# Attention with mixed heads and a two-layer network on one core: weight stores, x stores and norm's product change queues

## The chip, the core and the metric

The program runs on one core of a Trainium2 chip. The metric is the device time of one execution in microseconds (us). Five engines work from queues of their own and wait for each other through semaphores: TensorE (PE, with its weight loads PEld), VectorE (DVE), ScalarE (ACT), GpSimd (POOL) and SyncE (SP), which here only issues DMAs. GpSimd issues DMAs too, in the same queue as its arithmetic. Each queue is worked off in the order in which it is written.

## The reference

Four batches, 12 heads, 448 tokens, head size 64. Scores of all heads are mixed by a 12x12 matrix before the softmax and by another one behind it. The result, transposed to 1792 tokens x 768, goes through a two-layer network with a leaky activation. All of it is float32; the network's weights arrive as float64.

```python
scores = scale * np.matmul(q, k.transpose(0, 1, 3, 2))
scores = np.einsum('bhij,hg->bgij', scores, w_pre)
scores = scores - np.max(scores, axis=-1, keepdims=True)
attn = np.exp(scores)
attn = attn / (np.sum(attn, axis=-1, keepdims=True) + 1e-09)
attn = np.einsum('bhij,hg->bgij', attn, w_post)
return np.matmul(attn, v).astype(np.float32)
...
h = x @ w_in
g = np.maximum(h, 0.0) + alpha * np.minimum(h, 0.0)
return (g @ w_out).astype(np.float32)
```

## The kernel before

**Steps.** The attention is cut into 90 steps; the function `step(n)` writes the work of step n, for n from -1 to 94. In a step PE mixes the scores of 20 query rows over the heads (`mix`, L213), DVE takes their maxima (L215, once per step, so the instructions of this line count the steps), ACT takes the exponentials (L222), `norm` turns the sums of the step before into the second mixing matrix `r` (L229, L230 and the product L233, all on DVE), `post` (L246) mixes the result of two steps before with it, and `qk` (L185) makes the scores of a later chunk of queries in a tile `st`. Every few steps (8, 14, 20, 25, 29, 35, 41, 47 and so on) `pv` (L269, L283) multiplies by the values and leaves a piece of x in `xe`.

**Relays.** The scores are laid out anew on the way from `st` to six buffers `sr` by DMAs on SP's queue (L203, L206), three steps ahead of the `mix` that reads them.

**Conversion.** The weights are rounded from float64 to float32 in the kernel. `convert` works through 64 units (128x384 numbers each: 16 slices f, two matrices x, two halves), and each unit has five conversion operations: L60; L64 with L61 and L62 on GpSimd; L65; L66; L67. The others are DVE's. The first three of unit i stand ahead of the last two of unit i-1. GpSimd fetches the raw numbers into four buffers `cr` (L307) and a rounded half `ct` goes to the scratch `wsc` in DRAM by a store on SP's queue (L317). That store is kept in the list `ripe` and written by `flush` at the start of the next step, ahead of that step's relays. The fetch into the buffer that unit i leaves is written behind the unit's last operation.

**The network.** `moe(t)` is the network for batch t, in four phases. A phase runs through `l1` (first layer, L414, then `prelu` on DVE, L368 and L369) and `l2` (second layer, L448, added up on DVE in L383). Between the steps' own work `moe_work` writes as much of it as `PACE` says: matmuls worth 5000 ns in a step of the first phase. For each weight slice GpSimd loads the rounded numbers back (`load_w`, L352), ACT makes the high part (L360) and GpSimd the low part (L361). `load_w` writes further conversion operations on the spot while the slice that it needs isn't converted. The attention of batch t must be in DRAM (`x2`, stores L286) before `load_x` (L464, SP) fetches it and `split_x` (L474, L475, DVE) cuts it in two parts.

**Lead.** Up to step `ready[0]` = 26 there is no network work and each step holds `CONV_LEAD` = 6 conversion operations; behind it come `CONV_T0` of them in each step until all are done.

Of the kernel before, what the change touches and what calls it, by code (L numbers as in the profile page):

```python
# [8 lines left out]
F32 = mybir.dt.float32  # L9
# [5 lines left out]
ALU = mybir.AluOpType  # L15
# [31 lines left out]
CONV_LEAD, CONV_T0 = 6, 9  # L47
# [23 lines left out]
def talking_heads_prelu(ctx: ExitStack, tc: tile.TileContext, q, k, v, w_pre, w_post, mask, w_in, w_out, alpha, out):  # L71
# [154 lines left out]
    def norm(n):  # L226
        se = se_t.pop(n)
        s1 = sm.tile([128, 2], F32, tag="s1", name=f"s1{n}")
        nc.vector.tensor_scalar_add(s1, se, 1e-9)  # L229
        nc.vector.reciprocal(out=s1, in_=s1)  # L230
        r = rp.tile([128, 2, HP], F32, tag="r", name=f"r{n}")
        wf = wq.rearrange("p (o g) i -> p o (g i)", o=1)
        nc.vector.tensor_tensor(r, wf.to_broadcast([128, 2, HP]),  # L233
                                s1.rearrange("p (u o) -> p u o", o=1).to_broadcast([128, 2, HP]), ALU.mult)
        r_t[n] = r

# [53 lines left out]
    ripe = []  # L290

    def flush(upto=None):
        while ripe and (upto is None or ripe[0][0] <= upto or len(ripe) > 2):
            ripe.pop(0)[1]()
        now, later[:] = list(later), []
        for f in now:
            f()

    def convert():
        todo = [(f, x, c) for f in range(NFC) for x in range(2) for c in range(0, DM, CU)]  # L300
        raw_c = {}

        def fetch_c(i):
            if i < len(todo):
                f, x, c = todo[i]
                raw_c[i] = cvp.tile([128, CU], I64, tag="cr", bufs=4, name=f"cr{f}_{x}_{c}")
                nc.gpsimd.dma_start(out=raw_c[i], in_=(w_in, w_out)[x][f, :, c:c + CU])  # L307

        def unit(i):
            f, x, c = todo[i]  # L310
            raw = raw_c.pop(i)
            e = cvp.tile([128, CU], I32, tag="ce", name=f"ce{f}_{x}_{c}")
            t = cvp.tile([128, CU], I32, tag="ct", bufs=4, name=f"ct{f}_{x}_{c}")
            for j, op in enumerate(round_f64(nc, raw, e, t)):
                op()
                if j == 4:
                    ripe.append((step_now[0], lambda: (stored.add((f, x, c)), nc.sync.dma_start(  # L317
                        out=wsc[f, :, x * DM + c:x * DM + c + CU], in_=t.bitcast(F32)))))
                    fetch_c(i + 4)
                yield  # L320

        for i in range(2):
            fetch_c(i)
        yield
        n = len(todo)
        seq = []
        for i in range(n + 1):
            seq += [(i, 0), (i, 1), (i, 2)] if i < n else []
            seq += [(i - 1, 3), (i - 1, 4)] if i else []
        units = {}  # L330
        for i, j in seq:
            if j == 0:
                units[i] = unit(i)
            next(units[i], None)
            if i < 2 and j == 1:
                fetch_c(i + 2)
            yield

# [3 lines left out]
    soon = []  # L342

    def load_w(u, x):
        t, f = divmod(u, NFC)
        if t >= len(TB):
            return
        while not all((f, x, c) in stored for c in range(0, DM, CU)):
            converts(1)
            flush()  # L350
        w = (rip, rop)[x].tile([128, DM], F32, tag="r", name=f"wr{u}_{x}")
        nc.gpsimd.dma_start(out=w, in_=wsc[f, :, x * DM:(x + 1) * DM])  # L352
        wr_t[u, x] = w

# [45 lines left out]
    def moe(t):  # L400
# [3 lines left out]
        for what, G in order():  # L404
            fs = [FG * G + j for j in range(FG)]
            if what == "l1":
                pt = grab()
                for f in fs:
# [17 lines left out]
                    load_w(u + 4, 0)  # L426
# [40 lines left out]
    def split_x(t):  # L467
        a, N = TB[t]
        while step_now[0] < ready[t]:
            yield  # L470
        xs = xs_t[t] = xsp.tile([128, 2, NCC, N], F32R, tag="xs", name=f"xs{t}")
        for c in range(NCC):
            xr = xr_t.pop((t, c))
            nc.vector.tensor_copy(xs[:, 0, c, :], xr[:, :N])  # L474
            nc.vector.tensor_tensor(xs[:, 1, c, :], xr[:, :N], xs[:, 0, c, :], ALU.subtract)  # L475
            if c + 2 < NCC:
                load_x(t, c + 2)
            yield
# [20 lines left out]
    with tc.manual_schedule():  # L499
# [54 lines left out]
        conv_done, conv_steps = 0, NFC * 2 * 5 * (DM // CU)  # L554
# [10 lines left out]

        def moe_work(n, amount):
            nonlocal cur, budget
            budget += amount
            while budget > 0 and cur < len(TB):
                if tasks[cur] is None:  # L570
                    if n <= ready[cur]:
                        budget = 0.0
                        return
                    for _ in (nxt_x[cur] if cur in nxt_x else split_x(cur)):
                        pass
                    if cur == 1:
                        converts(conv_steps)
                        flush()
# [8 lines left out]
        def step(n):  # L587
# [6 lines left out]
            lead = n <= ready[0]  # L594
            pace = 0.0 if lead else PACE[min(cur, 2)]
            flush(n - 1)
            if live(n):
                mix(n)
            if n >= 0:
                relays(2 * (n + RA + 1), (nc.sync,))  # L600
            for f, *args in loads:
                f(*args)
# [22 lines left out]
            else:  # L625
                moe_work(n, pace * 0.5)
                converts(CONV_T0 // 2)
                moe_work(n, pace * 0.5)
                converts(CONV_T0 - CONV_T0 // 2)
            flush(n - 1)  # L630
            for t in range(len(TB)):
                if n == ready[t] - 1:
                    load_x(t, 0)
                    load_x(t, 1)
                if n == ready[t] and t == 0:
# [3 lines left out]
            if n == ready[0] - 5:  # L639
                for u in range(2):  # L640
                    for x in range(2):
                        load_w(u, x)
            if n == ready[0] - 2:
                for u in range(2):
                    split_w(u, 0)
                    load_w(u + 2, 0)
# [43 lines left out]
```

## Time and profile before

| | us |
|---|---|
| three runs | 992.94, 994.39, 999.21 |
| median | 994.39 |
| the profiled execution: its own time | 1000.09 |
| the profiled execution: span of the core | 998.30 |

The span is what the trace covers. It lies 1.79 us below that execution's own time and 3.91 us above the median of the runs. Times in the trace are counted from the start of the span. An instruction's row gives its start, its length and, in brackets, the idle time of its engine ahead of it with what ended that. The granted clock is TensorE's, as a share of 2.4 GHz.

### The profile page before, as it was taken

The page shows a single profiled execution, that of the slowest core. Times are in us where ns is not written, and L with a number is a line of the kernel's source. Part 1 is how long each engine was busy: PE and PEld are TensorE (multiplying, and loading weights), DVE is VectorE, ACT ScalarE, POOL GpSimd, SP SyncE. Part 2 cuts the span into 40 slices and gives each one's busy share as a digit, 9 for nine tenths or more (in the row PEclk, how much of TensorE's full clock was granted, in tenths as well). Part 3 has the DMA queues.
Part 4 walks back from the last instruction along what each step waited for, and adds up shares of the span by engine and source line. Part 5 has one row for each costly group of instructions (what it writes and reads, how often), then busy time and mean ns, then how long its engine had stood idle before and what let it go on. Part 6 is the DMA issues. An engine that isn't in the chain of part 4 may idle for free. (4 is left out here: it accounts for less than half of the span.)

```text
span 998.3 us, 27494 instructions
## 1 busy us (share of the span) xinstructions
PE 863.6 (87%) x11532; PEld 667.6 (67%) x11532; DVE 620.9 (62%) x1077; ACT 427.8 (43%) x780; POOL 488.9 (49%) x562
## 2 busy tenths in 40 slices
PE   6567747776978886997999989999999999999997
PEld 3235425445757654785787867777878888879997
DVE  4487947757987997744554544546655553654564
ACT  2255626513443442543555445554654545132231
POOL 6443634626556675451335434362533335367661
PEclk7699979967988997997999999999999999999999
DMA  6777877866666776454444464366534332544322
GB/s 185 184 241 215 244 211 227 234 205 179 194 180 198 224 214 180 140 161 147 156 136 136 123 163 128 117 181 195 167 116 122 118 106 80 160 127 125 111 80 72
DMA packets 79724, 161.73 MB, mean 162 GB/s; under 512 B 26276, under 2 KB 64304, under 8 KB 79600
## 3 DMA queue, kind: packets, MB, share of 16 engines
q0 software_dynamic: 21312, 90.58, 33.6%
q1 hardware_dynamic: 57432, 68.18, 21.1%
q8 instruction: 91, 1.49, 0.6%
q10 hardware_dynamic: 856, 1.21, 0.5%
q14 instruction: 33, 0.27, 0.1%
HBM read 97.62 MB, written 23.59 MB: 121 GB/s over the span
## 5 line engine op out<-in xcount | busy, mean ns | idle before, releaser
L361 POOL TENSOR_TENSOR ws<-wr,ws 128x768 fp32r<-128x768 f32 x128 | 237.1, 1853 | 294.2 <-ACT ws L360 287.0
L414 PE MATMUL p<-xs,ws 128*128 128x448 f32 x1152 | 261.7, 381 | 9.9 <-DVE xs L474 8.4
L448 PE MATMUL p<-g,ws 128*128 128x448 f32 x1152 | 253.5, 375 | 13.4 <-ACT e L222 5.9
L414 PEld LDWEIGHTS p<-xs,ws 128*128 128x128 f32 x1152 | 219.3, 194 | 55.5 <-issue 18.6
L448 PEld LDWEIGHTS p<-g,ws 128*128 128x128 f32 x1152 | 219.3, 193 | 50.0 <-ACT e L222 6.7
L215 DVE TENSOR_REDUCE nm<-p 128x2 f32<-128x896 f32 x90 | 97.6, 1085 | 115.4 <-PE p L213 115.4
L246 PEld LDWEIGHTS p<-r,e 64*64 64x64 f32 x5040 | 104.7, 139 | 81.7 <-issue 39.6
L252 ACT COPY at<-p 128x960 f32<-128x960 f32 x88 | 86.8, 987 | 168.5 <-PE p L246 168.4
L222 ACT ACTIVATE e<-p,nm 128x448 f32<-128x448 f32 x180 | 112.8, 635 | 100.8 <-DVE nm L215 68.5
L246 PE MATMUL p<-r,e 64*64 64x60 f32 x5040 | 109.6, 227 | 41.5 <-DVE xe L283 17.2
L360 ACT CAST ws<-wr 128x768 fp32r<-128x768 f32 x128 | 104.0, 843 | 95.8 <-issue 55.1
L185 PE MATMUL p<-k,q 64*64 64x448 f32 x768 | 110.8, 614 | 39.2 <-ACT st L189 13.4
L383 DVE TENSOR_TENSOR acc<-p,acc 128x896 f32<-128x896 f32 x84 | 91.0, 1086 | 61.0 <-PE p L448 60.9
L213 PE MATMUL p<-sr,wk 64*64 64x448 f32 (+1 forms) x720 | 106.8, 585 | 21.9 <-DMA sr<-st 16.2
L189 ACT COPY st<-p 128x896 f32<-128x896 f32 x95 | 84.5, 913 | 57.0 <-DMA sr<-st 26.9
L368 DVE TENSOR_SCALAR t<-p,alpha_sb 128x448 f32<-128x448 f32 x64 | 43.4, 678 | 97.0 <-PE p L414 97.0
L352 POOL DMA_DIRECT2D wr<-wsc x128 | 72.2, 564 | 39.3 <-POOL ws L361 34.1
L269 PEld LDWEIGHTS p<-at,v 64*64 64x64 f32 x2688 | 76.9, 134 | 11.2 <-issue 5.5
L269 PE MATMUL p<-at,v 64*64 64x120 f32 (+1 forms) x2688 | 78.9, 262 | 2.4 <-ACT st L189 1.8
L185 PEld LDWEIGHTS p<-k,q 64*64 64x64 f32 x768 | 30.2, 145 | 60.5 <-issue 18.5
L213 PEld LDWEIGHTS p<-sr,wk 64*64 64x64 f32 (+1 forms) x720 | 25.8, 137 | 64.5 <-issue 31.6
L61 POOL TENSOR_SCALAR ce<-ce 128x384 int32<-128x384 int32 x64 | 34.9, 546 | 50.4 <-DVE ce L60 48.6
(47 smaller groups left out, 670.1 us busy)
## 6 DMA issues: line engine op xcount, KB each, us to landing
wr<-wsc POOLq DMA_DIRECT2D x128, 384.0 KB, 3.8
sr<-st SPq DMA_DIRECT2D x332, 105.0 KB
cr<-in_w_in_dram POOLq DMA_DIRECT2D x32, 384.0 KB, 5.2
cr<-in_w_out_dram POOLq DMA_DIRECT2D x32, 384.0 KB, 4.7
wsc<-ct SPq DMA_DIRECT2D x64, 192.0 KB
xr<-x SPq DMA_DIRECT2D x24, 224.0 KB
out_dram<-acc SPq DMA_DIRECT2D x12, 448.0 KB
q<-in_q_dram POOLq DMA_DIRECT2D x54, 90.0 KB, 5.1
```

The source lines that it names most:

```text
L185: nc.tensor.matmul(pt[64 * cc:64 * cc + 64, r, :S], q_t[ci][h, (3 * cc + p) * cn + SR0 * cc:(3 * cc + p) * cn + SR0 * cc + 64], k_t[b, p][ ...
L213: nc.tensor.matmul(to[hf:hf + 64, u, :S], wk[r, :], g[r, :], start=True, stop=True)
L215: nc.vector.tensor_reduce(out=nm, in_=to[:, :, :S], axis=AX.X, op=ALU.max, negate=True)
L222: nc.scalar.activation(out=e_t[n][:, u], in_=m_t[n][:, u, :S], func=AF.Exp, bias=nm_t[n][:, u:u + 1], scale=1.0, accum_out=se_t[n][:, u:u ...
L246: nc.tensor.matmul(dst[:, :, HI * u:HI * u + HI], e[h, u, 64 * jb:64 * jb + 64], r[h, u].rearrange("p (h i) -> p h i", h=H), start=True, s ...
L252: nc.scalar.copy(at[:, :, col:col + 2 * GI].rearrange("p q (g i) -> p g q i", g=2), pt[:, :, :NS * GP].rearrange("p g (q i) -> p g q i", i ...
L269: nc.tensor.matmul(to[64 * t:64 * t + 64, r, cl * cn:(cl + 1) * cn], v_t[b, hx][pr, s, (2 * cl + t) * D:(2 * cl + t + 1) * D], a_t[pr, s, ...
L360: nc.scalar.copy(t[:, 0], w)
L361: nc.gpsimd.tensor_tensor(t[:, 1], w, t[:, 0], ALU.subtract)
L383: nc.vector.tensor_tensor(dst, pt[:, :, :N], dst, ALU.add)
L414: nc.tensor.matmul(pt[:, f % 2, :S], w[:, tw, c * 128:(c + 1) * 128], xs[:, tx, c, :], start=(j == 0), stop=(j == 3 * NCC - 1))
L448: nc.tensor.matmul(pt[:, d, :S], w[:, tw, (c + d) * 128:(c + d + 1) * 128], g[:, tg], start=(j == 0), stop=(j == 3 * FG - 1))
```

## The change

1. A rounded half is stored by GpSimd (`close`, L301 in the new file) instead of SP. The store and the fetch of the next raw numbers stand behind GpSimd's two exponent operations (L61, L62) of the unit that is begun next but one.
2. `norm` is written inside the function that writes the steps. While the first network phase lasts, its product runs on GpSimd (L575 in the new file).
3. `flush` now writes x's stores behind the step's relays, once in a step. `load_x` and `split_x` come one step later, and so does every network phase; for the later phases `load_x` is written at the first use.
4. Each step of the first phase holds 8 and 9 conversion operations by turns (4 + n % 2, then 4) instead of 9, and `ahead` loads first-layer weights three slices ahead instead of four while t is 0.

```diff
-CONV_LEAD, CONV_T0 = 6, 9
+CONV_LEAD, CONV_T0 = 6, 8
...
-    def flush(upto=None):
-        while ripe and (upto is None or ripe[0][0] <= upto or len(ripe) > 2):
-            ripe.pop(0)[1]()
+    def flush():
         now, later[:] = list(later), []
...
+            def close():
+                stored.add((f, x, c))
+                nc.gpsimd.dma_start(out=wsc[f, :, x * DM + c:x * DM + c + CU], in_=t.bitcast(F32))
+                fetch_c(i + 4)
+
             for j, op in enumerate(round_f64(nc, raw, e, t)):
                 op()
+                if j == 1 and shut:
+                    shut.pop(0)()
                 if j == 4:
-                    ripe.append((step_now[0], lambda: (stored.add((f, x, c)), nc.sync.dma_start(
-                        out=wsc[f, :, x * DM + c:x * DM + c + CU], in_=t.bitcast(F32)))))
-                    fetch_c(i + 4)
+                    shut.append(close)
                 yield
...
+    def ahead(upto):
+        while next_w[0] <= upto:
+            load_w(next_w[0], 0)
+            next_w[0] += 1
...
+                if G == NG2 - 1 and t + 1 < len(TB) and step_now[0] > ready[t + 1]:
+                    load_x(t + 1, 0)
+                    load_x(t + 1, 1)
...
-                    load_w(u + 4, 0)
+                    ahead(u + (3 if t == 0 else 4))
...
-        while step_now[0] < ready[t]:
+        while step_now[0] < ready[t] + 1:
             yield
+        for c in range(2):
+            if (t, c) not in xr_t:
+                load_x(t, c)
...
+            (nc.gpsimd if cur == 0 else nc.vector).tensor_tensor(r, wf.to_broadcast([128, 2, HP]),
+                                    s1.rearrange("p (u o) -> p u o", o=1).to_broadcast([128, 2, HP]), ALU.mult)
...
-            lead = n <= ready[0]
+            lead = n <= ready[0] + 1
...
-            flush(n - 1)
             if live(n):
                 mix(n)
             if n >= 0:
                 relays(2 * (n + RA + 1), (nc.sync,))
+            flush()
...
-                converts(CONV_T0 // 2)
+                converts(CONV_T0 // 2 + n % 2)
                 moe_work(n, pace * 0.5)
                 converts(CONV_T0 - CONV_T0 // 2)
-            flush(n - 1)
             for t in range(len(TB)):
-                if n == ready[t] - 1:
+                if n == ready[t] and t == 0:
                     load_x(t, 0)
                     load_x(t, 1)
-                if n == ready[t] and t == 0:
+                if n == ready[t] + 1 and t == 0:
                     for _ in split_x(0):
                         pass
```

**GpSimd in the lead.** GpSimd's queue in a stretch of the lead: `ce` are the exponents of a unit, `cr` its raw numbers, `ct` its rounded half, with the matrix (0 or 1) and the half (0 or 384) behind the name; `r` is norm's product. Before:

```order
L307 DMA cr_0_384_1105<-in_w_in_dram 128x384
L61 TENSOR_SCALAR ce_1_384_1107<-ce_1_384_1107 128x384
L62 TENSOR_SCALAR ce_1_384_1107<-ce_1_384_1107 128x384
L307 DMA cr_1_0_1116<-in_w_out_dram 128x384
L168 DMA q_125<-in_q_dram 64x2x90 x2
```

After:

```order
L575 TENSOR_TENSOR r_998<-wq,s_995 128x120
L61 TENSOR_SCALAR ce_1_0_1040<-ce_1_0_1040 128x384
L62 TENSOR_SCALAR ce_1_0_1040<-ce_1_0_1040 128x384
L301 DMA wsc<-ct_0_0_908 128x384
L292 DMA cr_0_0_1047<-in_w_in_dram 128x384
```

The fetches into `cr` stood ahead of the exponent operations of the unit that is begun next. They now stand behind them and behind a store, and each step's product stands between.

**DVE in step 41.** DVE's queue in the middle of step 41, up to the first activation of `prelu` (L368 before, L364 after). Before:

```order
L60 TENSOR_SCALAR ce_0_384_4484<-cr_0_384_4285 128x384
L64 TENSOR_SCALAR ct_0_384_4485<-cr_0_384_4285 128x384
L65 SCALAR_TENSOR_TENSOR ct_0_384_4485<-cr_0_384_4285,ct_0_384_4485 128x384
L66 SCALAR_TENSOR_TENSOR ce_0_0_4457<-cr_0_0_4252,ce_0_0_4457 128x384
L67 TENSOR_TENSOR ct_0_0_4458<-ct_0_0_4458,ce_0_0_4457 128x384
L60 TENSOR_SCALAR ce_1_0_4494<-cr_1_0_4455 128x384
L64 TENSOR_SCALAR ct_1_0_4495<-cr_1_0_4455 128x384
L65 SCALAR_TENSOR_TENSOR ct_1_0_4495<-cr_1_0_4455,ct_1_0_4495 128x384
L66 SCALAR_TENSOR_TENSOR ce_0_384_4484<-cr_0_384_4285,ce_0_384_4484 128x384
L67 TENSOR_TENSOR ct_0_384_4485<-ct_0_384_4485,ce_0_384_4484 128x384
L368 TENSOR_SCALAR t_10_4506<-p_128,alpha_sb 128x448
L369 SCALAR_TENSOR_TENSOR t_10_4506<-p_128,t_10_4506 128x448
```

After, from the last conversion operation of step 41 on:

```order
L67 TENSOR_TENSOR ct_0_384_4236<-ct_0_384_4236,ce_0_384_4235 128x384
L215 TENSOR_REDUCE nm_4428<-p_129 128x2
L571 TENSOR_SCALAR s_4436<-se_4375 128x2
L572 RECIPROCAL s_4436<-s_4436 128x2
L60 TENSOR_SCALAR ce_1_384_4497<-cr_1_384_4385 128x384
L64 TENSOR_SCALAR ct_1_384_4498<-cr_1_384_4385 128x384
L65 SCALAR_TENSOR_TENSOR ct_1_384_4498<-cr_1_384_4385,ct_1_384_4498 128x384
L66 SCALAR_TENSOR_TENSOR ce_1_0_4390<-cr_1_0_4217,ce_1_0_4390 128x384
L364 TENSOR_SCALAR t_10_4522<-p_131,alpha_sb 128x448
L365 SCALAR_TENSOR_TENSOR t_10_4522<-p_131,t_10_4522 128x448
L364 TENSOR_SCALAR t_11_4525<-p_131,alpha_sb 128x448
L365 SCALAR_TENSOR_TENSOR t_11_4525<-p_131,t_11_4525 128x448
```

Before, the rows ahead of L368 are the end of a run of 17 conversion operations in step 41, 13 of which `load_w` asked for, and `prelu` waits behind all of them. After, the same `prelu` falls in step 42 and four conversion operations stand between norm's reciprocal and it.

**SP at the first hand-over.** SP's queue around the hand-over of batch 0: stores of x (`x`<-`xe`), loads of it (`xr`<-`x`), relays (`sr`<-`st`). Before:

```order
L286 DMA x_57<-xe_1_2365 128x3x28
L464 DMA xr_0_2422<-x_57 128x448
L464 DMA xr_1_2424<-x_57 128x448
L317 DMA wsc<-ct_1_0_2167 128x384
L203 DMA sr_121<-st_2011 60x1x448 x2
L203 DMA sr_122<-st_2011 60x1x448 x2
L464 DMA xr_2_2497<-x_57 128x448
```

After:

```order
L275 DMA x_57<-xe_1_2363 128x3x28
L463 DMA xr_0_2487<-x_57 128x448
L463 DMA xr_1_2489<-x_57 128x448
L203 DMA sr_117<-st_2228 60x1x448 x2
L203 DMA sr_118<-st_2228 60x1x448 x2
L463 DMA xr_2_2570<-x_57 128x448
```

Before, a store of a rounded half and four relays stood between the first two loads and the third. After, no store of a rounded half is left on the queue, and all of it comes one step of relays later.

## Rows read from the trace of the kernel before

**Rows 1.** The page's slices: busy tenths of DVE, granted clock of PE.

```profile
DVE  4487947757987997744554544546655553654564
...
PEclk7699979967988997997999999999999999999999
```

**Rows 2.** Windows by stage: us, busy us of each engine, clock, DMA share, GB/s.

```profile
0.00:195.10 195.10, 130.42 (x2596) 75.26 (x2596) 131.32 (x294) 90.92 (x177) 96.31 (x163) 0.86 0.76 216
195.10:216.60 21.50, 12.43 (x88) 6.09 (x88) 11.27 (x23) 3.08 (x6) 6.50 (x11) 0.58 0.83 259
216.60:400.80 184.20, 145.09 (x1943) 111.95 (x1943) 161.28 (x269) 71.88 (x132) 114.50 (x147) 0.88 0.65 189
400.80:428.90 28.10, 28.10 (x350) 21.33 (x351) 18.31 (x31) 16.26 (x30) 10.89 (x10) 1.00 0.47 140
```

**Rows 3.** Waits of PE, 216.6 to 400.8: us in total, times, longest.

```profile
PE p L246 <- DVE xe L283: 17.2, 3, 9.4
PE p L185 <- DVE t L369: 11.7, 3, 6.0
PE p L448 <- ACT e L222: 5.9, 2, 4.2
```

**Rows 4.** DVE by line, 216.6 to 400.8: count, busy, mean ns, idle before.

```profile
L67 DVE TENSOR_TENSOR ct<-ct,ce 128x384 f32<-128x384 f32 x30 | 26.8, 893 | 0.8
L66 DVE SCALAR_TENSOR_TENSOR ce<-cr,ce 128x384 int32<-128x384 int32 x30 | 23.3, 777 | 4.5 <-POOL ce L62 4.5
L65 DVE SCALAR_TENSOR_TENSOR ct<-cr,ct 128x384 f32<-128x384 uint32 x30 | 22.6, 755 | 0.9
L60 DVE TENSOR_SCALAR ce<-cr 128x384 int32<-128x384 int32 x30 | 18.5, 615 | 0.8
...
L64 DVE TENSOR_SCALAR ct<-cr 128x384 int32<-128x384 int32 x30 | 13.0, 432 | 0.0
```

**Rows 5.** Timeline, DVE and GpSimd at 190 us: start, length, instruction.

```profile
190.34 2.44 DVE L66 SCALAR_TENSOR_TENSOR ce<-cr,ce 128x384 int32<-128x384 int32 x1
192.81 0.56 DVE L67 TENSOR_TENSOR ct<-ct,ce 128x384 f32<-128x384 f32 x1
...
190.51 1.84 POOL L361 TENSOR_TENSOR ws<-wr,ws 128x768 fp32r<-128x768 f32 x1
```

**Rows 6.** Timeline, PE in step 41.

```profile
396.15 1.77 PE L185 MATMUL p<-k,q 64*64 64x448 f32 x8 [5.96 <-DVE t L369]
```

**Rows 7.** DVE by line, 0 to 195.1: the product, the reuse of ct.

```profile
L64 DVE TENSOR_SCALAR ct<-cr 128x384 int32<-128x384 int32 x33 | 12.1, 365 | 8.4 <-DMA wsc<-ct 8.3
L233 DVE TENSOR_TENSOR r<-wq,s 128x120 f32<-128x120 f32 x25 | 7.1, 283 | 0.9
```

**Rows 8.** GpSimd by line, 216.6 to 400.8.

```profile
L361 POOL TENSOR_TENSOR ws<-wr,ws 128x768 fp32r<-128x768 f32 x22 | 41.5, 1887 | 22.4 <-ACT ws L360 16.3 <-DMA sr<-st 5.3
L62 POOL TENSOR_SCALAR ce<-ce 128x384 int32<-128x384 int32 x30 | 18.6, 619 | 2.5
...
L352 POOL DMA_DIRECT2D wr<-wsc x22 | 12.8, 580 | 8.8 <-POOL ws L361 4.8 <-DMA wsc<-ct 3.8 <-DMA x<-xe 0.3
```

**Rows 9.** Timeline: fetch of unit 21, unit 19's L62, first use (L60).

```profile
113.79 0.57 POOL L307 DMA_DIRECT2D cr<-in_w_in_dram  x1 [1.42 <-DVE ce L66]
...
115.23 0.70 POOL L62 TENSOR_SCALAR ce<-ce 128x384 int32<-128x384 int32 x1
...
122.58 0.36 DVE L60 TENSOR_SCALAR ce<-cr 128x384 int32<-128x384 int32 x1
```

**Rows 10.** DMA issues, 0 to 195.1: count, KB each, median us to landing.

```profile
cr<-in_w_in_dram POOLq DMA_DIRECT2D x18, 384.0 KB, 5.7
...
wsc<-ct SPq DMA_DIRECT2D x30, 192.0 KB
```

**Rows 11.** DMA issues, 216.6 to 400.8, the same fetch.

```profile
cr<-in_w_in_dram POOLq DMA_DIRECT2D x13, 384.0 KB, 4.9
```

**Rows 12.** Timeline of DVE at the first hand-over.

```profile
204.87 0.39 DVE L474 CAST xs<-xr 128x448 fp32r<-128x448 f32 x1 [4.30 <-DMA xr<-x]
```

More of the change, by code (lines that the diff above doesn't have):

```diff
@@ L224, in exp @@
         free(m_t.pop(n))
[L226 to L235, printed above, removed]
     def post(n):
@@ L288, in pv @@
                 in_=xe[:, :3 * cn].rearrange("p (c i) -> p c i", c=3)[:, :, o + skip:o + w]))
-    ripe = []
-    def flush(upto=None):
-        while ripe and (upto is None or ripe[0][0] <= upto or len(ripe) > 2):
-            ripe.pop(0)[1]()
+    def flush():
         now, later[:] = list(later), []
@@ L300, in convert @@
         todo = [(f, x, c) for f in range(NFC) for x in range(2) for c in range(0, DM, CU)]
-        raw_c = {}
+        raw_c, shut = {}, []
         def fetch_c(i):
@@ L337, in convert @@
             yield
+        for f in shut:
+            f()
     wr_t, wi_t, wo_t, g_t, xs_t, xr_t = {}, {}, {}, {}, {}, {}
     nxt_x, stored = {}, set()
-    soon = []
+    soon, next_w = [], [0]
     def load_w(u, x):
@@ L349, in load_w @@
             converts(1)
-            flush()
         w = (rip, rop)[x].tile([128, DM], F32, tag="r", name=f"wr{u}_{x}")
@@ L553, in talking_heads_prelu @@
         next(conv)
-        conv_done, conv_steps = 0, NFC * 2 * 5 * (DM // CU)
+        conv_done, conv_steps = 0, NFC * 2 * 5 * (DM // CU) + 1
         tasks = [None] * len(TB)
@@ L564, in converts, with norm @@
                     conv_done += 1
+        def norm(n):
+            se = se_t.pop(n)
+            s1 = sm.tile([128, 2], F32, tag="s1", name=f"s1{n}")
+            nc.vector.tensor_scalar_add(s1, se, 1e-9)
+            nc.vector.reciprocal(out=s1, in_=s1)
+            r = rp.tile([128, 2, HP], F32, tag="r", name=f"r{n}")
+            wf = wq.rearrange("p (o g) i -> p o (g i)", o=1)
+            (nc.gpsimd if cur == 0 else nc.vector).tensor_tensor(r, wf.to_broadcast([128, 2, HP]),
+                                    s1.rearrange("p (u o) -> p u o", o=1).to_broadcast([128, 2, HP]), ALU.mult)
+            r_t[n] = r
         def moe_work(n, amount):
@@ L570, in moe_work @@
                 if tasks[cur] is None:
-                    if n <= ready[cur]:
+                    if n <= ready[cur] + 1:
                         budget = 0.0
@@ L577, in moe_work @@
                         converts(conv_steps)
-                        flush()
                         cvs.close()
@@ L639, in step @@
             if n == ready[0] - 5:
+                ahead(1)
                 for u in range(2):
-                    for x in range(2):
-                        load_w(u, x)
+                    load_w(u, 1)
             if n == ready[0] - 2:
@@ L645, in step @@
                     split_w(u, 0)
-                    load_w(u + 2, 0)
+                ahead(2)
         for n in range(-1, NB + LAG + 3):
```

## The prediction

> **What bounds the kernel now.** I read the page's slices first [rows 1]. The clock falls below full speed in most of the first sixteen slices (400 us) and almost nowhere behind them, so TensorE is kept waiting there and bounds the rest. The windows by stage [rows 2] say by whom. From 216.6 to 400.8 us, the first network phase while weights are still being converted, DVE is busy 161.3 of 184.2 us and PE 145.1. In the 28.1 us behind it, with the conversions over, PE is busy all of the time and DVE 18.3. The lead, up to 195.1, is mixed: DVE 131.3, PE 130.4, with 0.76 of the DMA engines taken. The interval between maxima that holds the first hand-over, 195.1 to 216.6, is the emptiest, with PE 12.4 of 21.5 us at a clock of 0.58.
>
> The waits of PE in the first phase [rows 3] are all for DVE or for ACT, which waits for DVE: xe 17.2 us, prelu's t 11.7, exponentials 5.9. No relay and no weight is among them. So a gain from SP's queue, where the change moves most DMAs, can't be read from this stage, and one from DVE's order and load can.
>
> **The price of a conversion operation.** In this stage DVE's five operations take 893, 777, 755, 615 and 432 ns [rows 4], 694 ns in the mean, and there are 30 of each: 150 operations in 15 steps (27 to 41), ten a step, though nine are written. The rest came by load_w.
>
> **Part 1, the spread of the conversions.** By the code the lead of before holds 28 x 6 = 168 of the 320 operations. The new lead has one step more, 174 of 321 (one is the end of the list). The remaining 147 go into steps 28 to 45 at 8.5 a step and load_w asks for none, since it finds its slices stored: 8.2 a step over 18 steps against 10 over 15. That takes 1.8 x 0.69 = 1.25 us of DVE's time from each step. A step of before is 184.2 / 15 = 12.28 us; I take 11.03 for the new one, so the 18 steps last 198.5 us. They begin one lead step later than 216.6; DVE is busy 131.3 / 26 = 5.05 us a step in the lead [rows 2], so 221.7 us. That puts the maximum of step 46 at 420.2 us. Before it stands at 428.9, but the network is a step further there, 5.0 us of matmuls by PACE, so 423.9 is the like of it: -3.7 us. The average leaves out the worst step. In step 41 seventeen conversion operations stand ahead of prelu, and PE waits 5.96 us for its t [rows 6], with the low clock behind it (slice 16 stands at 7 tenths) [rows 1]. In the new order four stand there. I count -5 for that: the wait, less about 1 us since conversions reappear in steps 42 to 45. DVE has the room: 18.3 of 28.1 us were busy [rows 2], 4.6 us a step, and 8.5 x 0.69 = 5.9 more makes 10.5, below 11.03. Sum -9. Bounds: if DVE's 22.9 idle us of this stage (184.2 - 161.3) all went, the step would be 161.3 / 15 - 1.25 = 9.5, less than PE's 145.1 / 15 = 9.67, and 18 x 9.67 gives -28 in all. If nothing of the smaller load showed but the longer stretch, 18 x 11.6 gives +7.
>
> **Part 2, norm's product on GpSimd.** 51 products leave DVE, 283 ns each in the lead [rows 7]. What they cost GpSimd has no row. By size from L361 [rows 8], 120 of 768 elements of 1887 ns are 295 ns; the upper bound is L62, 619 ns, which has 384. What DVE pays for it does have one: while L361 runs on GpSimd (190.51, 1.84 us) L66 takes 2.44 us, against 0.56 for L67 right behind it, clear of L361 [rows 5]. So a product of two tiles on GpSimd holds up DVE's work between SBUF tiles for as long as it lasts, and the operations behind the reciprocal are such work. DVE wins 283 ns and loses 0 to 500. I take a gain of 0.05 us on the 40 or so that lie in DVE-bound steps: -2, range -11 to +9. GpSimd itself has room: 114.5 of 184.2 us [rows 2], and 15 x (0.45 + 1.7 stores of 0.58, the price of L352 in rows 8) adds 21 us. It is on the path only if its waits add up.
>
> The Trainium skill (SBUF — State Buffer, section SBUF: two separate sides) has this as a lock that one of the two engines holds for a whole instruction; L66 in rows 5 agrees. By that rule alone, with every product locked out against a waiting DVE for 0.3 us, part 2 would be about 0 instead of -2.
>
> **Part 3, the later fetch.** This is a cost. Before, the raw numbers of unit 21 are asked for at 113.79 and first used at 122.58, 8.8 us later [rows 9]. In the new order the fetch stands behind unit 19's L62, which ends at 115.93, and behind a store (0.58): 116.5, which leaves 6.1 us. The median landing in the lead is 5.7 [rows 10], and now 192 KB of a store lie directly ahead of the 384 KB in the same queue. Bounds of the landing: 5.7, and 5.7 x 1.33 = 7.6 if the queue is one line and half of the two share their time. I take 6.6. A shortfall x must be made up by the nine conversion operations between fetch and use, so each unit's five stretch by 5x/9. With x = 0.5 and about 20 units (the lead holds 35; the others lie in steps that wait for something else) that is +6; with x = 0 it is 0 and with x = 1.5 it is +17. In the first phase the operations are slower and the landing shorter, 4.9 [rows 11], so I count nothing there.
>
> The skill's same section warns that DMAs issued by GpSimd starve, since their descriptors can't be written while DVE holds the port. It would lengthen these landings and move the sum to the first rival. The trace doesn't bear it out: DVE is busier from 216.6 on (0.88 against 0.67 of the time) and the landing is shorter there [rows 2, 10, 11].
>
> **Part 4, SP without rounded halves.** DVE waited 8.3 us in the lead for stores to clear ct [rows 7], five times. The store now leaves as soon as GpSimd gets to it and ten operations ahead of the reuse, so the wait goes. Most of it fell in steps that waited for something else anyway: -3, range -8 to 0.
>
> **Part 5, the hand-over.** The stores of x, its loads and the split all move one step, so their distances stay. DVE waits 4.30 us for the first piece [rows 12]. The loads are now a step behind the loads of v that are issued in step 25: -1, range -4 to +3. In the later hand-overs SP gets to the load later, but DVE has idle time there; 0, range -3 to +3.
>
> **Sum.** -9 - 2 + 6 - 3 - 1 = -9. The durations are of an execution of 1000.09 us, 5.7 above the median of 994.39. The differences carry over, so 994.4 - 9 = **985 us**.
>
> **Rivals.** (a) **The fetch binds the lead.** If the landing in the lead, with a store ahead, exceeds 7.6 us, x is above 1.5, part 3 costs 17 us or more, and the sum is +2 to +6: about **999**, slower than before. For it: the margin of 6.1 is within 0.4 of the median. Against it: DVE stretches by itself when DMAs are late. It decides from x = 1.3 on. (b) **The first phase evens out.** If most of DVE's 22.9 idle us go with the runs of conversions, because PE no longer falls to the low clock (0.88 in this stage), part 1 is -20 and the time **974**. For it: PE's waits of 17.2 and 11.7 us are three long ones each, the mark of runs and not of a steady lack. Against it: the steps with pv remain uneven. (c) **Nothing comes of it.** GpSimd's product and stores push its L62 behind, DVE waits for it (4.5 us before, rows 4), and the lost time equals what the spread gives: **994**.
>
> **How the numbers follow.** One per cent, 9.9 us, is about what a measurement of this kernel tells from no change. Chances: the forecast 0.40 (979 to 991), (a) 0.20, (b) 0.22, (c) 0.18. Faster by over 1% (below 984.5): (b) and half of the forecast, 0.42. Slower by over 1% (above 1004.3): a part of (a) with the upper ends of parts 1 and 2, 0.12. Within: 0.46. The range 968 to 1003 takes in the cases' centres and most of the bounds of part 1 below and of part 3 above.
>
> **What would show it.** Right: L215 of step 46 near 420 us; no wait of PE for prelu's t above 3 us; the five DVE operations at 10 operations a step fewer than before and still near 0.69 us; no DVE wait for wsc; the hand-over a step later but as long. Part 3 shows as idle time of L60 released by the cr loads, 5 to 6 us more than before; 15 us more is rival (a). Wrong: L66, L65 or L60 in the lead well above their means of before would say that the product on GpSimd costs DVE more than it saves; idle time of L66 released by L62 is rival (c).

## The result and the profile after

The changed kernel takes 1006.65 us (median of 4 runs, 1001.82 to 1011.01), the kernel before 996.02 in the same comparison. The ratio is 1.0103, 95% interval 1.0071 to 1.0136: slower by 10 us, where 985 was forecast and 1003 was the upper end. The profiled execution took 1011.01 us, its span 1009.2. Ratios here and below are of fast runs alone (1000.83 us of o4_four_if_stored and 1100.07 and 4041.30 of b_spread_alone are left out), medians of all runs.

The windows by stage, which answer to [rows 2], with the same columns. The second fence holds the stretch behind step 46 of the kernel before, which [rows 2] don't have. The lead now ends with step 27, the hand-over is 197.2 to 217.1, and steps 28 to 45 fill 217.1 to 431.9.

```profile
0.00:192.50 192.50, 129.31 (x2580) 80.19 (x2582) 128.59 (x269) 91.06 (x176) 125.36 (x217) 0.86 0.74 218
...
217.10:431.90 214.80, 175.46 (x2244) 132.55 (x2244) 169.30 (x268) 84.17 (x156) 146.85 (x204) 0.91 0.61 178
431.90:1009.20 577.30, 551.03 (x6535) 456.36 (x6533) 300.87 (x462) 244.13 (x434) 263.46 (x239) 0.98 0.45 131
```

```profile
428.90:998.30 569.40, 547.52 (x6572) 452.99 (x6564) 298.66 (x465) 245.69 (x435) 260.68 (x232) 0.98 0.46 132
```

Step 28's maximum falls at 217.1, 4.6 us earlier than the 221.7 of the prediction. The lead is not where the time went. Then 18 steps take 214.8 us, 11.93 each, against a forecast of 11.03 and an upper bound of 11.6: 16 us too much in one stage. DVE is idle 45.5 us of it (214.8 - 169.30), against 22.9 of 184.2 before, though its load was to be the limit. Behind step 46 the rest is 577.3 us, 569.4 before; 5.0 of the 7.9 us is, by PACE, the step of network work that was put off.

So the stage is read again, by its waits. Waits in 217.1 to 431.9 of the changed kernel, mainly those of ScalarE and DVE (us in total, times, longest):

```profile
ACT e L222 <- DVE nm L215: 41.8, 8, 15.0
ACT ws L356 <- DMA wr<-wsc: 39.0, 6, 6.7
DVE g L371 <- ACT g L370: 31.6, 6, 6.1
...
PE p L447 <- ACT at L241: 19.3, 6, 3.8
...
DVE t L364 <- PE p L413: 4.3, 2, 4.0
```

The first row is the largest, but it isn't new: it stood at 36.2 us before, and most of its longest wait, 15.0, lies ahead of 217.1. The second row is the new one. ScalarE waits 39.0 us for loads of weights, six times. In the stage of before the same casts waited for GpSimd alone and never for a load, by their row for 216.6 to 400.8:

```profile
L360 ACT CAST ws<-wr 128x768 fp32r<-128x768 f32 x22 | 17.8, 844 | 8.4 <-POOL ws L361 8.4
```

DVE now waits for ScalarE's g, six times too. One of the six, in step 33, in the timelines of ScalarE, GpSimd and DVE (start, length, instruction, idle time ahead and what ended it):

```profile
282.69 0.85 ACT L356 CAST ws<-wr 128x768 fp32r<-128x768 f32 x1
290.10 0.83 ACT L356 CAST ws<-wr 128x768 fp32r<-128x768 f32 x1 [6.56 <-DMA wr<-wsc]
290.84 1.03 ACT L370 CAST g<-t 128x448 fp32r<-128x448 f32 x2
291.77 0.97 ACT L241 COPY at<-p 128x960 f32<-128x960 f32 x1
...
283.62 1.82 POOL L357 TENSOR_TENSOR ws<-wr,ws 128x768 fp32r<-128x768 f32 x1 [0.35 <-ACT ws L356]
285.37 0.60 POOL L343 DMA_DIRECT2D wr<-wsc  x1
...
285.17 1.08 DVE L379 TENSOR_TENSOR acc<-p,acc 128x896 f32<-128x896 f32 x1
291.43 2.42 DVE L371 TENSOR_TENSOR g<-t,g 128x448 fp32r<-128x448 f32 x2 [5.18 <-ACT g L370]
```

Read it from the load. It is issued at 285.37, behind GpSimd's L357 of the slice before, and the cast that reads it starts 4.7 us later, at 290.1. That cast is the next one on ScalarE's queue and has waited since 283.5. Behind it stand `prelu`'s two casts g (L370) and the copy of at (L241), which need nothing of that load. DVE has finished L379 at 286.25 and stands still 5.18 us for g, with norm's and the conversions' work queued behind L371. TensorE's wait for at (19.3 us, six times) is the end of the chain. The cause in the code is the last line of the change: `ahead(u + 3)` asks for a slice right behind the cast of the one before. `l1` takes the slices in pairs, and in all six cases nothing stands on ScalarE's queue between the two casts of a pair. With four ahead the load had a whole pair's time. The buffer is not what holds the load up: there are two by turns, L357 has just left the other one, and the row at 285.37 has no wait. Only the order in the code, the load behind `split_w`, puts it there; no run tried the load ahead of it.

The rows that answer to the prediction's other marks. First two of DVE's conversion operations in the stage, by line:

```profile
L66 DVE SCALAR_TENSOR_TENSOR ce<-cr,ce 128x384 int32<-128x384 int32 x30 | 24.1, 804 | 0.4 <-POOL ce L62 0.4
L67 DVE TENSOR_TENSOR ct<-ct,ce 128x384 f32<-128x384 f32 x30 | 23.9, 796 | 0.8
```

Then the lead, 0 to 192.5: TensorE's longest wait in sum, DVE by line, and GpSimd by line.

```profile
PE p L235 <- POOL r L575: 24.0, 11, 3.6
```

```profile
L66 DVE SCALAR_TENSOR_TENSOR ce<-cr,ce 128x384 int32<-128x384 int32 x32 | 25.7, 802 | 0.0
...
L60 DVE TENSOR_SCALAR ce<-cr 128x384 int32<-128x384 int32 x33 | 12.6, 382 | 30.1 <-DMA cr<-in_w_out_dram 16.2 <-DMA cr<-in_w_in_dram 13.4
```

```profile
L575 POOL TENSOR_TENSOR r<-wq,s 128x120 f32<-128x120 f32 x25 | 11.7, 468 | 19.3 <-DVE s L572 19.1
```

The operations of the stage cost what was assumed (804 and 796 ns; 777 and 893 in [rows 4]). The product takes 468 ns on GpSimd, not the 295 that I scaled from L361. L60 waits 29.6 us for raw numbers in the lead, three times the 9.8 of the kernel before (5.4 and 4.4, one wait each).

### The profile page after: what moved, and what is told of

Its sections match the earlier page's. It is cut to its first block, busy times and chain, and to the rows that moved or that the text cites. A ratio compares the mean times of both kernels' runs of the same rounds, so it can differ in the third digit from the quotient of the medians.

```text
span 1009.2 us, 27411 instructions
## 1 busy us (share of the span) xinstructions
PE 871.5 (86%) x11532; PEld 677.3 (67%) x11532; DVE 613.5 (61%) x1026; ACT 427.2 (42%) x780; POOL 546.2 (54%) x677
## 4 chain that ended last, share of the span: by engine, by line
PE 52%; DMA 17%; DVE 11%; POOL 8%; issue 6%; ACT 5%; SPq 1%; POOLq 0%; ACTq 0%; DVEq 0%
PE p L413 18%; PE p L447 16%; PE p L258 6%; PE p L213 4%; PE p L235 4%; DMA sr<-st 4%; DMA wr<-wsc 4%; POOL ws L357 3%; DMA cr<-in_w_out_dram 3%; PE p L185 3%; DMA xr<-x 3%; DVE nm L215 2%; ACT ws L356 1%; DVE g L371 1%; DMA cr<-in_w_in_dram 1%
## 5 line engine op out<-in xcount | busy, mean ns | idle before, releaser
L357 POOL TENSOR_TENSOR ws<-wr,ws 128x768 fp32r<-128x768 f32 x128 | 236.3, 1847 | 274.1 <-ACT ws L356 272.7
L447 PE MATMUL p<-g,ws 128*128 128x448 f32 x1152 | 259.8, 381 | 31.0 <-ACT at L241 20.6
L447 PEld LDWEIGHTS p<-g,ws 128*128 128x128 f32 x1152 | 221.4, 195 | 69.3 <-ACT at L241 25.4
L215 DVE TENSOR_REDUCE nm<-p 128x2 f32<-128x896 f32 x90 | 97.6, 1084 | 96.4 <-PE p L213 90.2
L241 ACT COPY at<-p 128x960 f32<-128x960 f32 x88 | 86.5, 983 | 140.3 <-PE p L235 140.1
L185 PE MATMUL p<-k,q 64*64 64x448 f32 x768 | 106.2, 588 | 20.5 <-DMA k<-in_k_dram 6.6
L379 DVE TENSOR_TENSOR acc<-p,acc 128x896 f32<-128x896 f32 x84 | 90.9, 1085 | 50.9 <-PE p L447 50.8
L364 DVE TENSOR_SCALAR t<-p,alpha_sb 128x448 f32<-128x448 f32 x64 | 43.4, 678 | 90.8 <-PE p L413 90.8
L258 PEld LDWEIGHTS p<-at,v 64*64 64x64 f32 x2688 | 81.7, 140 | 15.7 <-issue 5.9
L258 PE MATMUL p<-at,v 64*64 64x120 f32 (+1 forms) x2688 | 84.2, 272 | 6.3 <-ACT st L189 3.6
L371 DVE TENSOR_TENSOR g<-t,g 128x448 fp32r<-128x448 f32 x64 | 65.5, 1063 | 38.7 <-ACT g L370 38.7
L61 POOL TENSOR_SCALAR ce<-ce 128x384 int32<-128x384 int32 x64 | 35.5, 554 | 51.6 <-DVE ce L60 48.7
```

The source lines that it names most:

```text
L185: nc.tensor.matmul(pt[64 * cc:64 * cc + 64, r, :S], q_t[ci][h, (3 * cc + p) * cn + SR0 * cc:(3 * cc + p) * cn + SR0 * cc + 64], k_t[b, p][ ...
L215: nc.vector.tensor_reduce(out=nm, in_=to[:, :, :S], axis=AX.X, op=ALU.max, negate=True)
L241: nc.scalar.copy(at[:, :, col:col + 2 * GI].rearrange("p q (g i) -> p g q i", g=2), pt[:, :, :NS * GP].rearrange("p g (q i) -> p g q i", i ...
L258: nc.tensor.matmul(to[64 * t:64 * t + 64, r, cl * cn:(cl + 1) * cn], v_t[b, hx][pr, s, (2 * cl + t) * D:(2 * cl + t + 1) * D], a_t[pr, s, ...
L357: nc.gpsimd.tensor_tensor(t[:, 1], w, t[:, 0], ALU.subtract)
L379: nc.vector.tensor_tensor(dst, pt[:, :, :N], dst, ALU.add)
```

## The experiments

Theory A: the six late loads are the loss, since ScalarE's queue holds prelu's g behind them. Rival B: GpSimd's fuller queue makes them late, whatever the distance. Rival C: the loss lies in the lead, in norm's product or in the later hand-overs. a4, b3, o4 (short for o4_four_if_stored and the like) and p3 tell these apart, o4_prelu_first joins two of the edits, and the others take parts of the prediction, by themselves or from the best version. Differences between kernels below are differences of ratios times 995 us; with intervals of about 0.3% on each ratio they are good to some 4 us.

| kernel | median us | ratio to the kernel before (95%) |
|---|---|---|
| the change | 1006.65 | 1.0103 (1.0071 to 1.0136) |
| a4_four_ahead | 1000.04 | 1.0052 (1.0029 to 1.0076) |
| b3_before_three_ahead | 1007.90 | 1.0122 (1.0081 to 1.0163) |
| o4_four_if_stored | 991.98 | 0.9968 (0.9941 to 0.9995) |
| o4_norm_on_vector | 993.29 | 0.9982 (0.9957 to 1.0007) |
| p3_prelu_first | 989.81 | 0.9953 (0.9931 to 0.9976) |
| o4_prelu_first | 988.58 | 0.9917 (0.9887 to 0.9947) |
| b_spread_alone | 991.30 | 0.9962 (0.9942 to 0.9983) |
| o4_early_fetch | 987.19 | 0.9922 (0.9898 to 0.9947) |
| best_all_three | 981.16 | 0.9859 (0.9817 to 0.9901) |
| best_norm_on_vector | 979.74 | 0.9840 (0.9805 to 0.9876) |
| best_stores_on_sp | 987.57 | 0.9911 (0.9877 to 0.9945) |
| spread_prelu_first | 986.51 | 0.9908 (0.9872 to 0.9944) |

**a4_four_ahead.**

```diff
-                    ahead(u + (3 if t == 0 else 4))
+                    ahead(u + 4)
...
-                ahead(2)
+                ahead(3)
```

> The changed kernel, with first-layer weights loaded four slices ahead in the first phase too (as before), all else as changed. Theory A (loads three ahead make every second cast on ScalarE wait for its load, 39.0 us in 6 waits, and prelu's g on DVE behind it, 31.6 us): the six waits of L356 for wr fall below 5 us in sum, DVE's for g too. Each of the six steps loses some 5.3 us less, 32 in all, but load_w now asks for conversions again (12 operations in one step, 23 in another, against 8 and 9), which I put at +7: about 982, range 974 to 992. Rival B (GpSimd's queue, fuller by stores and products, is what makes the loads late): waits of L356 stay above 20 us, time 998 to 1007. Rival C (the loss lies in the lead, norm's product or the later hand-overs): the stage changes by under 8 us, time above 998.

1000.04 us: 5 us less than the change, not 24. ScalarE's waits for wr are gone from the stage, as theory A says and rival B doesn't. The time alone, above 998, would have fitted rivals B and C as well; against C stands the stage, steps 28 to 45, which takes 203.0 us instead of 214.8. But `load_w` asks for conversions again, 12 operations in step 39 and 23 in step 42, and their price, 7 us, was put too low. TensorE in the timeline of that step:

```profile
379.79 0.63 PE L235 MATMUL p<-r,e 64*64 64x60 f32 x26
395.39 1.77 PE L185 MATMUL p<-k,q 64*64 64x448 f32 x8 [14.97 <-DVE t L365]
```

It waits 14.97 us for prelu's t, and the step takes 25.4 us (373.9 to 399.3, L215 to L215). A run of 22 stood in step 41 of the kernel before [rows 6], with a wait of 5.96, and that step took 24.8 us too (375.9 to 400.8), so the wait alone was no measure of it. Nor is the long step: the steps behind it are short in return (5.4 and 5.8 us here), since hardly a conversion is left. So the three slices of the change do save something: the run. Both have a price.

**b3_before_three_ahead.** The same edit the other way round, alone in the kernel before: `ahead` and its 3.

```diff
-                    load_w(u + 4, 0)
+                    ahead(u + (3 if t == 0 else 4))
...
                     split_w(u, 0)
-                    load_w(u + 2, 0)
+                ahead(2)
```

> The kernel before with this one part of the change: first-layer weights loaded three slices ahead while t is 0. load_w then asks for no conversions, nine operations stand in every step up to 45, none has 22. Theory A: six waits of ScalarE for wr of 4 to 7 us appear, DVE waits for g behind them, 5 us each, less some 6 us for the run of 22 operations that is gone: 1010 to 1025, about 1016. Rivals B and C: no such waits, and the time stays at 990 to 998 (lower if the run of operations in step 41 was a cost by itself).

1007.90 us, 12 us above the kernel before and just under the range given (1010 to 1025). The six waits appear in a kernel whose GpSimd has no stores and no product, so rivals B and C fall as the main cause (213.5 to 437.4, steps 27 to 45):

```profile
ACT ws L365 <- DMA wr<-wsc: 31.0, 6, 6.8
...
DVE g L380 <- ACT g L379: 18.4, 6, 6.5
```

This one line of the change, by itself, costs as much as the whole change does.

**o4_four_if_stored.** Four ahead where the slice is already converted, three where it isn't: no run, and late loads only in the last two pairs.

```diff
+    def have(u):
+        return all((u % NFC, 0, c) in stored for c in range(0, DM, CU))
...
-                    ahead(u + (3 if t == 0 else 4))
+                    ahead(u + (4 if t or have(u + 4) else 3))
...
-                ahead(2)
+                ahead(3)
```

> The changed kernel, loading four slices ahead wherever the fourth is already converted and three otherwise, so load_w asks for no conversions and the load is late only in the last two pairs of slices. Theory A: two waits of L356 are left of six, 10 to 14 us; 4 x 5.3 = 21 us less than the changed kernel: about 985, range 977 to 992. Rivals B and C: above 998. Against a4_four_ahead it tells whether runs of conversions or late loads cost more: by part 1 of the prediction the run of 23 costs 5 and two late loads 10, so this one should be no more than 5 us away.

991.98 us, 13 less than the change; theory A in kind, two thirds of it in size. It is 8.4 us under a4, where at most 5 was expected, so runs of conversions cost more than I had put on them. Two waits are left, as counted:

```profile
ACT ws L359 <- DMA wr<-wsc: 12.1, 2, 6.5
DVE g L374 <- ACT g L373: 10.4, 2, 6.3
```

A wait was worth 3.4 us and not 5.3. Step 33 shows why. It fell from 16.7 us to 13.3. The 5.18 us of idle time are gone, since g comes at once (L374 starts at 281.52, behind L382), but L67 behind it runs into GpSimd's next L360:

```profile
283.79 3.06 DVE L67 TENSOR_TENSOR ct<-ct,ce 128x384 f32<-128x384 f32 x1
...
284.58 1.85 POOL L360 TENSOR_TENSOR ws<-wr,ws 128x768 fp32r<-128x768 f32 x1
```

From g to the next L60 DVE takes 5.4 us here (281.52 to 286.89) and 3.5 in the changed kernel (291.43 to 294.94), where the next L357 lies beside g itself. So 1.9 of the 5.2 us come back as longer operations. The stage says the same of all four loads: DVE's idle time falls from 45.5 us to 25.7, its busy time rises from 169.3 to 174.4.

**o4_norm_on_vector.** The product on DVE in all phases.

```diff
-            (nc.gpsimd if cur == 0 else nc.vector).tensor_tensor(r, ...
+            nc.vector.tensor_tensor(r, ...
```

> As o4_four_if_stored, with norm's product on DVE through all phases as before. By part 2 of the prediction the product on GpSimd gains 2 us (range -11 to +9), so this kernel should be 2 us slower than o4. Rival: in the lead TensorE waits 25.5 us for r on GpSimd, against 10.8 us for r on DVE before, and GpSimd's queue stands 22.7 us behind r in the first phase; then this kernel is 5 to 12 us faster than o4.

1.4 us above o4, well inside the intervals; on the best version (below) it is 1.9 us under it. The product's engine makes no difference that these runs show.

**p3_prelu_first.** Three ahead as in the change, so all loads stay late, but what stands behind the late cast moves ahead of it (first phase only).

```diff
+                    if f == fs[-1] and t == 0:
+                        prelu(t, fs, pt)
                     split_w(u + 2, 0)
                     ahead(u + (3 if t == 0 else 4))
-                    if f == fs[-1]:
+                    if f == fs[-1] and t:
                         prelu(t, fs, pt)
```

> The changed kernel (three slices ahead), but in the first phase prelu is written ahead of the cast of the late slice, so that its g on ScalarE no longer stands behind the cast that waits. Theory A (what costs is the work behind a late load on ScalarE's queue, not the load as such): ScalarE's waits for wr stay near 35 us in six, DVE's for g fall from 31.6 to under 6, and the time falls by most of what four_if_stored gave, 10 to 20 us: about 991, range 985 to 997. Rival: the next exponentials and the copies of at stand behind the same cast, so the loss only moves to them, and the time stays within 5 us of 1006.6.

989.81 us: 15 us less than the change, with every load written where it was. This is the direct test of the queue's order. ScalarE still waits for wr (in 218.6 to 408.9, steps 28 to 45), though 16.0 us and not the 35 expected, since it now comes to the cast later. DVE has no wait for g in that stretch, and nothing of that size took its place:

```profile
ACT at L241 <- PE p L235: 17.7, 8, 6.0
...
ACT ws L356 <- DMA wr<-wsc: 16.0, 5, 3.8
...
ACT g L370 <- DVE t L365: 9.6, 13, 1.9
```

The rival, by which the loss moves to the exponentials, falls: TensorE waits 3.4 us for e in L449 and 6.7 for at, no more.

**o4_prelu_first.** Both edits.

> Both: four ahead where stored, and prelu ahead of the cast. o4_four_if_stored kept two of six waits, 12.1 us, with DVE's for g of 10.4; four waits less gave 14.7 us, 3.7 each, so the two that are left are worth 7: about 985, range 981 to 990. Rival (the two late waits are covered by PE's own work, since steps 42 and 45 end the stage): same as o4_four_if_stored, 990 to 994.

988.58 us, 5 under o4, for the two late loads that were left. From here to a4 it is 13.4 us, about twice the 7 that were put on a4's runs.

**b_spread_alone.** The kernel before with 8 and 9 conversion operations by turns and o4's rule for the loads.

```diff
-CONV_LEAD, CONV_T0 = 6, 9
+CONV_LEAD, CONV_T0 = 6, 8
...
-                converts(CONV_T0 // 2)
+                converts(CONV_T0 // 2 + n % 2)
...
-                    load_w(u + 4, 0)
+                    ahead(u + (4 if t or have(u + 4) else 3))
```

> The kernel before with part 1 alone: 8 and 9 conversion operations by turns, and four slices ahead where stored, else three, so that load_w asks for at most one. Norm, stores, fetch and hand-over as before. By part 1 of the prediction 9 us less than before, with two or three late loads at 3.7 us each on top: about 995 - 9 + 9 = 995, range 988 to 999; L215 of step 46 at 428 or earlier. Rival (the spread gives nothing by itself, and the gain of four_if_stored over the kernel before comes from the moved queues): 1000 to 1006, since the late loads then stand alone.

991.30 us, 4 under the kernel before, at the lower part of the range, with L215 of step 46 at 423.9 instead of 428.9. In 216.0 to 423.9 two late loads are left (11.7 us in ScalarE's waits).

**o4_early_fetch.** The fetch of raw numbers back behind the unit's last operation; the store stays on GpSimd behind the exponents.

```diff
             def close():
                 ...
-                fetch_c(i + 4)
...
                     shut.append(close)
+                    fetch_c(i + 4)
```

> As o4_four_if_stored, but the fetch of the next raw numbers stands where it stood before, right behind a unit's last operation, ahead of the exponents and the store. By part 3 of the prediction the later fetch costs 6 us (0 to 17), all in the lead: this kernel 986, range 980 to 992, and L60's waits for cr in the lead fall from over 30 us to about 10. Rival: the waits fall as said, but the lead's steps wait for relays and for r all the same, and GpSimd stands waiting for DVE's L66 at each fetch again: within 3 us of o4, 989 to 995.

987.19 us, 5 under o4. DVE in 0 to 192.5 of this kernel:

```profile
L60 DVE TENSOR_SCALAR ce<-cr 128x384 int32<-128x384 int32 x34 | 14.1, 414 | 12.1 <-DMA cr<-in_w_out_dram 6.2 <-DMA cr<-in_w_in_dram 5.1
L64 DVE TENSOR_SCALAR ct<-cr 128x384 int32<-128x384 int32 x34 | 12.8, 376 | 9.4 <-DMA wsc<-ct 9.3
```

L60's waits fall from 30.1 us (the change) to 12.1, and a wait for stores to clear ct comes back that the late fetch had covered. Of 18 us of waits, 9 moved, and the time follows by 5. Where those 5 lie I can't say: by one profile each the lead ends 1.0 us earlier and the stage behind it is 5.0 shorter, and such stages differ by some us between executions.

**best_all_three.** o4_prelu_first with the early fetch.

> The changed kernel with the three mended places together: four slices ahead where stored, prelu ahead of the cast in the first phase, and the fetch of raw numbers right behind a unit's last operation. o4_prelu_first gave 988.6, and the early fetch took 4.8 from o4_four_if_stored: 984, range 980 to 988, faster than the kernel before by about 1.1%. Rival: prelu's order and the early fetch remove the same idle time, and it stays at 987.

981.16 us, 1.4% under the kernel before, and 24 us under the change. Steps 28 to 45 take 183.6 us of it, 10.2 each. The clock in the 40 slices, of the changed kernel and of this one; slices 10 to 18 now stand at 9, where the changed kernel has five of these nine below it:

```profile
PEclk7798978879899878988999999999999999999999
```

```profile
PEclk7699978769999999997999999998999999989999
```

**best_norm_on_vector.**

> As best_all_three, with norm's product on DVE in all phases. Part 2 of the prediction: 2 us slower than best_all_three; o4_norm_on_vector was 1.3 us slower than o4, less than its interval. So 984 to 988. Rival (r on GpSimd delays post in the lead by more than it takes off DVE): 978 to 983.

979.74 us: 1.9 us under best_all_three, within the intervals. This is the fastest kernel by its median, with one move less.

**best_stores_on_sp.** Stores kept in a list and written at the start of the next step on SP, as before.

```diff
-                nc.gpsimd.dma_start(out=wsc[f, :, ...
+                nc.sync.dma_start(out=wsc[f, :, ...
...
-                    shut.append(close)
+                    ripe.append((step_now[0], close))
...
+            release(n - 1)
             if live(n):
                 mix(n)
```

> As best_all_three, with the rounded halves stored through SP's queue at the start of the next step, as before. Part 4 of the prediction: 3 us slower than best_all_three (0 to 8), with DVE's waits for a store to clear ct in the lead; 987, range 984 to 992. Rival: the waits lie in steps that wait for relays anyway, and GpSimd is freed of 64 issues of 0.6 us: within 2 us of best_all_three or faster.

987.57 us, 5 above best_all_three, between the value (3) and the bound (8) of part 4. The reason is not the one that I wrote. DVE's waits for stores to clear ct are alike in 0 to 222, 9.0 us with the stores on GpSimd and 8.3 with them on SP. The first of these rows is of best_all_three, the second of best_stores_on_sp:

```profile
PE p L213 <- DMA sr<-st: 12.8, 9, 4.3
```

```profile
PE p L213 <- DMA sr<-st: 12.3, 2, 10.5
```

With stores ahead of the relays on SP, TensorE waits once 10.5 us for a relay, between the maxima of steps 2 and 3; without them the longest wait is 4.3. But the sums are alike, and that interval is only 2.2 us longer (15.3 against 13.1), so the relays are not shown to be the cause either. It stays open. The stage behind the lead is as long in both (183.6 and 185.3 us), and the lead ends at 215.7 and 220.4.

**spread_prelu_first.** The kernel before with b_spread_alone's edits and prelu first; no queue is changed.

> The kernel before with the spread, four ahead where stored, and prelu ahead of the cast, but no queue changed: norm on DVE, stores on SP, fetch and hand-over as before. Against best_all_three it gives parts 2, 4 and 5 together, which the prediction puts at -6: if so 990, and best_all_three is 6 us faster. Rival (only the order of conversions, loads and prelu bears on the time, and the moved queues give nothing): b_spread_alone's 991.3 less some 6 for the three late loads, 984 to 987, level with best_all_three.

986.51 us, 5 above best_all_three. So parts 2, 4 and 5 give 5 us together (with the fetch early), and the order of conversions, loads and prelu gives 9 without any of them. Not run is the kernel before with prelu's order alone: `prelu` stands there behind the conversions that `load_w` asks for, so some of the 9 may be that order's and not the spread's.

## Why the prediction was wrong

The step that failed is one that the prediction doesn't have. Item 4 of the change stands in the diff with its two lines, and the sum has no term for "loads first-layer weights three slices ahead instead of four". Part 1 takes its good side, "load_w asks for none", and no side that costs. Its price with all that hangs on it is the way from o4_prelu_first to the change, 18.5 us: 13.4 for four late loads of six and 5.1 for the two that remain, or the queue's order around them. As the only edit (b3) it costs 12 us, with the run of conversions saved.

The rows to see it by were there. A load took 4.2 us in the median in that stage of the kernel before, and [rows 8] has its issue (L352, 0.58 us) behind L361, which needs the cast before. With one slice of distance the next cast stands 0.85 us behind. What follows on ScalarE's queue is in `l1`: `prelu` is written behind `split_w`.

The terms that the prediction has hold in size, in the versions where the late loads are out of the way:

- **Part 1**, -9 (-28 to +7): spread_prelu_first is 9.2 us under the kernel before, b_spread_alone, with two late loads, 3.8. How much of that is the spread's and how much prelu's order is not shown. In o4, with two late loads, a step takes 11.1 us (200.1 / 18), forecast 11.03; in best_all_three 10.2. Two of its marks were right too: no wait of TensorE for t above 3 us in the changed kernel's stage, the five operations at 0.67 us in the mean (98.5 us for 146). The third was not: step 46 came at 431.9 and not near 420.
- **Part 2**, -2 (-11 to +9): -1.4 and +1.9 us in two tries, no difference. The product is longer than scaled (468 ns, 283 on DVE), TensorE waits 24.0 us for r in the lead, 6.9 before, and L66 takes 802 ns there, 713 before; DVE has 51 products less. The Trainium skill (GPSIMD Engine Reference, section 4.1 Engine selection) puts elementwise work with two inputs on GpSimd at about twice DVE's time; here it is 1.65.
- **Part 3**, +6 (0 to +17): 4.6 us in o4, 5.8 in the best version. The mark was wrong: L60's waits grew by 20 us, four times the price, which would have spoken for rival (a). Against that rival stands the lead's end, 4.6 us ahead of the forecast. A wait in a step that waits for something else is no measure of time.
- **Part 4**, -3 (-8 to 0): -5.2 us, but not through DVE's waits for ct, which are alike with either queue; the cause is open.
- **Part 5**, -1: not tried by itself. The interval with the hand-over is 20.0 us, 21.5 before, a step later, as forecast.

By spread_prelu_first (-9.2), then to best_all_three (-4.9), to o4_prelu_first (+5.8) and to the change (+18.5) the sum is +10.2, the change's ratio; the first three, -8.3, are the -9 that was forecast. That the parts add up is built into such a chain; that three of its steps come out at their forecast size is not, though each is good to some 4 us only and the first has prelu's order in it.

Rival (a) had the sign and of the four cases the nearest time (999), but by luck: its mechanism, the fetch in the lead, costs 5 us and not 17. Rival (b) falls for the change, where DVE's idle time in the stage grew (22.9 us in 15 steps before, 45.5 in 18); what it describes is seen in best_all_three, with 9.7 us idle of 183.6 and the clock at 0.97 there. Rival (c) falls: L66 waits 0.4 us for L62 in the stage. What stays open is the part behind step 46, 2.9 us longer than the step that was put off explains; no run isolates the later hand-overs. One reading was off, without effect on the sum: in [rows 1] eight of the first sixteen slices stand below 9 tenths, half of them and not most.

The Trainium skill (PSUM — Partial Sum Buffer, section Engine vs sequencer instructions) says that the queues of ScalarE, VectorE and GpSimd are strictly first in, first out. p3_prelu_first shows what that is worth here: 15 us for the order of two lines, with the late loads left as they were.

## What to carry to other kernels

Count a prefetch distance in time, not in slices: the issue waits for its buffer or for what stands ahead of it on its queue, the load takes its 4 to 5 us, and between two uses that stand close together there is nothing to hide it. Where one instruction on an in-order queue may wait for a DMA, look at what is written behind it that doesn't need the DMA, and write that first. And give every line of a diff a term in the sum, be it a zero with the work that covers it.

## What was not expected of the hardware

A late load cost less than the wait that it causes: 3.4 us of time for a wait of 6.5 on ScalarE and 5.2 on DVE, since with the load in time DVE's operations run into GpSimd's product of the next slice (L67 takes 3.06 us instead of about 0.6). In o4 this is the rule: up to 432 us, 14 of DVE's conversion operations take over 1.3 us, and each of them ends 0.2 to 0.4 us behind the end of such a product. And 30 stores more on GpSimd's queue in the lead, 0.6 us each, had no clear effect on when its own fetches land: 5.1 and 6.3 us in the median (the two matrices), 5.7 and 5.1 before.
